# A decode layer's last tile: result halves spread over four quadrants, the last tile in a PSUM tile of its own

## The chip, the cores and the metric

The kernel runs on one core of one Trainium2 chip. The metric is the time of one execution in device microseconds; times are medians of several executions.

## What is computed

One token's layer: a normalized input goes through attention over a window of 4096 cached keys and values (32 query heads, 4 key heads) and through a gated GELU block, and both are added to the input.

```python
x = A_x                                   # [1, 1, 1024]
xn = _layernorm(x, axis=-1)
return x + _A_ref(xn, A_k_cache, A_v_cache, A_wq, A_wo) + _B_ref(xn, B_w_gate, B_w_up, B_w_down)

# _A_ref ends in   o.reshape(1, 1, 4096) @ wo            wo:     [4096, 1024]
# _B_ref ends in   (gelu(x @ w_gate) * (x @ w_up)) @ w_down     w_down: [3584, 1024]
```

All is float32. The result row has 1024 elements and is the sum of x, 4096 rows of wo and 3584 rows of w_down, each weighted by one number.

## The kernel before

Every weight is read once from HBM, as a stream of 24 items (`items`), each of which fills a buffer `chunk` of up to 4 MB; there are four such buffers, so an item is loaded four items ahead, as soon as PE and DVE are done with the buffer's old content. The order of the instructions is that in which the code is written (`manual_schedule`): each engine takes its own in that order, and waits for what it reads.

The change lies in the last eight items: four of wo (kind "o") and four of w_down (kind "d"), of 8 row groups each, 4 in the last. A row group, called a tile t here, is 128 rows of the weight by 1024 columns. A tile is added to the result in one of two ways, in `contract`:
- PE (`accumulate`): four matmuls, one for each quadrant of 32 partitions of the PSUM tile `out_p`. Quadrant c takes 256 columns of the tile, c * 256 to c * 256 + 255 (CO is 256), so `out_p` holds the result row in four pieces in the partitions 0, 32, 64 and 96. A float32 matmul of the code is two MATMUL instructions on the chip, so a tile is eight.
- DVE (`add_scaled`): the tile, scaled by one factor per partition, is added to `out_part`, 128 x 1024 in SBUF. At tile MERGE = 20 of w_down, PE sums `out_part` over the partitions into `out_p` (the matmuls `out_p<-out_part,unit`; called the merge).

Even tiles go to PE and odd ones to DVE, except that from tile 16 of w_down on all go to PE. w_down has 28 tiles, 0 to 27. Tiles 16 to 19 and 20 to 23 are one transfer each (`TAIL`), 24, 25 and 26 one each, and tile 27, the last, comes in two transfers of 512 columns: quadrants 0 and 1 read the first, 2 and 3 the second. Behind it DVE adds `out_p` and `x_out`, the input in the same four pieces (line 453), and SP stores the four pieces (line 454):

```python
nc.vector.tensor_add(y, out_p, x_out)
nc.sync.dma_start(out.rearrange("a b (c n) -> (a b c) n", n=CO), y[0:P:32, :])
```

Of the kernel before, what the change touches and what calls it, by code (L numbers as in the profile page):

```python
# [9 lines left out]
F32 = mybir.dt.float32  # L10
# [5 lines left out]
P = 128  # L16
# [9 lines left out]
CO = D // 4  # L26
TD = DF // P
GROUP = 8
# [3 lines left out]
MERGE = 20  # L32
# [7 lines left out]
def tile_decode_layer(  # L40
# [12 lines left out]
    nc = tc.nc  # L53
    consts = ctx.enter_context(tc.tile_pool(name="consts", bufs=1))
    stream = ctx.enter_context(tc.tile_pool(name="stream", bufs=4))
    work = ctx.enter_context(tc.tile_pool(name="work", bufs=1))
    psum = ctx.enter_context(tc.tile_pool(name="psum", bufs=1, space=PSUM))
# [53 lines left out]
    nc.scalar.dma_start(x_rows, x.rearrange("a b (j p) -> (a b j) p", j=NJ))  # L111
    x_out = work.tile([P, CO], F32, name="x_out")
    nc.vector.memset(x_out, 0.0)
    nc.scalar.dma_start(x_out[0:P:32, :], x.rearrange("a b (c n) -> (a b c) n", n=CO))

    ident = consts.tile([P, P], F32, name="ident")
    make_identity(nc, ident)
# [11 lines left out]
    unit = consts.tile([P, 32], F32, name="unit")  # L129
# [51 lines left out]
    def add_scaled(total, w, factor, first):  # L181

        if first:
            nc.vector.tensor_scalar(total, w, factor, None, op0=ALU.mult)  # L184
        else:
            nc.vector.scalar_tensor_tensor(total, w, factor, total, op0=ALU.mult, op1=ALU.add)  # L186
# [196 lines left out]

    out_p = psum.tile([P, CO], F32, name="out_p", tag="out")
    out_part = work.tile([P, D], F32, name="out_part")

    def accumulate(z, w, start, stop):
        for c in range(4):
            nc.tensor.matmul(  # L389
                out_p[32 * c:32 * c + 32, :], z, w[:, c * CO:(c + 1) * CO], start=start, stop=stop  # L390
            )

    def contract(kind, a, z, count):
        w = loaded.pop((kind, a))
        for i in range(min(GROUP, count - GROUP * a)):
            t = GROUP * a + i
            wt = w[:, i * D:(i + 1) * D]
            if kind == "d" and t == MERGE:
                accumulate(unit, out_part, False, False)
            if i % 2 == 0 or (kind == "d" and t >= MERGE - GROUP // 2):  # L400
                accumulate(z[:, t, :], wt, kind == "o" and t == 0, kind == "d" and t == count - 1)
            else:
                add_scaled(out_part, wt, z[:, t, 0:1], kind == "o" and t == 1)

# [5 lines left out]
    for n, (kind, i) in enumerate(items):  # L410
# [15 lines left out]
        elif kind == "v":  # L426
            vn = loaded.pop(("v", i))
            half = STREAM // 2
            values(2 * i, vn[:, :half])
            values(2 * i + 1, vn[:, half:])  # L430
            if i == 1:
                maxima()
        elif kind in "gu":
            project(kind, i, NA)
            if (kind, i) == ("u", 1):
                state = factors()
            elif (kind, i) == ("u", 2):
                normalizers(*state)
                heads()
        elif kind == "o":  # L440
            if i == 0:
                projected("u", NA)
                gated()
            contract("o", i, oz, HQ)
            if i == 0:
                hidden()
        else:
            contract("d", i, hz, TD)
        if n + ahead < len(items):
            load(n + ahead)  # L450

    y = work.tile([P, CO], F32, name="y")
    nc.vector.tensor_add(y, out_p, x_out)
    nc.sync.dma_start(out.rearrange("a b (c n) -> (a b c) n", n=CO), y[0:P:32, :])


_INS = ["A_x", "A_k_cache", "A_v_cache", "A_wq", "A_wo", "B_w_gate", "B_w_up", "B_w_down"]
# [20 lines left out]
```

## Time and profile before

| | |
|---|---|
| median of 3 runs | 229.94 us (229.8 to 229.94) |
| the profiled execution | 229.72 us |
| its span, first to last instruction | 227.9 us |
| PE, DVE, ACT busy | 123.2, 97.0, 33.3 us |
| HBM read, over the span | 94.38 MB, 414 GB/s |
| last add, last store issued | 224.72 us, 225.17 us |

The span is shorter than the time by what lies around the first and the last instruction, 1.8 us. Times in the rows are counted from the start of the span. PEld is PE's loading of weights, which overlaps PE. SPq is SP's queue, which issues the transfers. In a matmul the small operand of 32 columns (`hz`, `oz`, `unit`) is loaded, and the weight tile streams through.

### The profile page before, as it was taken

The page shows a single profiled execution, that of the slowest core. Times are in us where ns is not written, and L with a number is a line of the kernel's source. Part 1 is how long each engine was busy: PE and PEld are TensorE (multiplying, and loading weights), DVE is VectorE, ACT ScalarE, POOL GpSimd, SP SyncE. Part 2 cuts the span into 40 slices and gives each one's busy share as a digit, 9 for nine tenths or more (in the row PEclk, how much of TensorE's full clock was granted, in tenths as well). Part 3 has the DMA queues.
Part 4 walks back from the last instruction along what each step waited for, and adds up shares of the span by engine and source line. Part 5 has one row for each costly group of instructions (what it writes and reads, how often), then busy time and mean ns, then how long its engine had stood idle before and what let it go on. Part 6 is the DMA issues. An engine that isn't in the chain of part 4 may idle for free.

```text
span 227.9 us, 2497 instructions
## 1 busy us (share of the span) xinstructions
PE 123.2 (54%) x1096; PEld 60.6 (27%) x1096; DVE 97.0 (43%) x103; ACT 33.3 (15%) x57; POOL 0.7 (0%) x6
## 2 busy tenths in 40 slices
PE   1160622567679834269806985384875425063754
PEld 1110000144364701017305472110571202021331
DVE  7340724520204164260380227966817356292600
ACT  2000000054273400006316350000000000000000
POOL 1000000000000000000000000000000000000000
PEclk9999999599958996577975899959655556675879
DMA  7989999999999999999999999999999999999991
GB/s 277 455 380 454 460 391 443 411 456 436 393 440 461 410 410 453 401 438 451 400 428 449 428 424 441 428 443 403 440 454 405 437 449 414 431 443 391 436 378 47
DMA packets 4786, 94.53 MB, mean 415 GB/s; under 512 B 540, under 2 KB 552, under 8 KB 1192
## 3 DMA queue, kind: packets, MB, share of 16 engines
q1 hardware_dynamic: 4760, 94.38, 97.1%
q8 instruction: 8, 0.13, 0.2%
q14 instruction: 2, 0.02, 0.0%
q10 hardware_dynamic: 16, 0.01, 0.0%
HBM read 94.38 MB, written 0.00 MB: 414 GB/s over the span
## 4 chain that ended last, share of the span: by engine, by line
DMA 57%; PE 22%; DVE 11%; ACT 6%; issue 2%; SPq 0%; ACTq 0%; DVEq 0%
DMA chunk<-in_A_k_cache 23%; DMA chunk<-in_B_w_down 15%; DMA chunk<-in_A_wo 14%; PE kt_p L241 8%; DMA chunk<-in_A_wq 5%; PE o_p L278 3%; DVE part L186 3%; PE s_p L250 3%; PE out_p L389 3%; PE acc_q L196 2%; DVE out_part L186 2%; DVE m L253 2%; ACT kT L242 2%; ACT p L256 2%; ACT pT L273 1%
## 5 line engine op out<-in xcount | busy, mean ns | idle before, releaser
L186 DVE SCALAR_TENSOR_TENSOR part<-chunk,xz,part 128x3584 f32<-128x3584 f32 (+1 forms) x9 | 37.1, 4126 | 32.1 <-DMA chunk<-in_A_wq 17.8
L241 PE MATMUL kt_p<-ident,chunk 128*128 128x128 f32 x128 | 23.7, 354 | 15.9 <-ACT kT L242 13.1
L242 ACT ACTIVATE kT<-kt_p 128x512 f32<-128x512 f32 x32 | 18.2, 596 | 70.9 <-PE kt_p L241 70.9
L196 PE MATMUL acc_q<-chunk,xz 128*32 128x512 f32 x64 | 14.3, 1043 | 24.0 <-DMA chunk<-in_A_wq 24.0
L241 PEld LDWEIGHTS kt_p<-ident,chunk 128*128 128x128 f32 x128 | 18.6, 180 | 24.8 <-ACT kT L242 16.2
L389 PE MATMUL out_p<-chunk,hz 128*32 128x256 f32 x160 | 14.8, 530 | 16.5 <-DMA chunk<-in_B_w_down 16.5
L186 DVE SCALAR_TENSOR_TENSOR out_part<-chunk,oz,out_part 128x1024 f32<-128x1024 f32 x15 | 19.3, 1285 | 10.4 <-DMA chunk<-in_A_wo 10.0
L389 PE MATMUL out_p<-chunk,oz 128*32 128x256 f32 x128 | 13.1, 580 | 15.7 <-DMA chunk<-in_A_wo 15.7
L196 PE MATMUL acc_g<-chunk,xz 128*32 128x512 f32 x56 | 10.9, 817 | 11.6 <-DMA chunk<-in_B_w_gate 11.6
L253 DVE TENSOR_REDUCE m<-s_p 128x1 f32<-128x1024 f32 x4 | 4.9, 1222 | 22.0 <-PE s_p L250 22.0
L186 DVE SCALAR_TENSOR_TENSOR out_part<-chunk,hz,out_part 128x1024 f32<-128x1024 f32 x8 | 10.3, 1284 | 9.1 <-DMA chunk<-in_B_w_down 8.9
L389 PEld LDWEIGHTS out_p<-chunk,hz 128*32 128x32 f32 x160 | 6.7, 147 | 24.6 <-DMA chunk<-in_B_w_down 12.5
L196 PEld LDWEIGHTS acc_q<-chunk,xz 128*32 128x32 f32 x64 | 2.5, 159 | 34.2 <-DMA chunk<-in_A_wq 23.3
L389 PEld LDWEIGHTS out_p<-chunk,oz 128*32 128x32 f32 x128 | 5.2, 156 | 23.2 <-DMA chunk<-in_A_wo 18.5
L196 PE MATMUL acc_u<-chunk,xz 128*32 128x512 f32 x56 | 9.4, 713 | 2.6 <-DMA chunk<-in_B_w_up 2.6
L278 PE MATMUL o_p<-chunk,pT 128*32 128x128 f32 x256 | 7.8, 274 | 1.9 <-ACT pT L273 1.9
L250 PE MATMUL s_p<-kT,qz 128*32 128x512 f32 x64 | 8.7, 612 | 0.0
L184 DVE TENSOR_SCALAR part<-chunk,xz 128x3584 f32<-128x3584 f32 (+1 forms) x3 | 6.5, 2169 | 3.9 <-DMA chunk<-in_A_wq 3.9
L278 PEld LDWEIGHTS o_p<-chunk,pT 128*32 128x32 f32 x256 | 6.7, 110 | 2.9 <-ACT pT L273 2.9
L196 PEld LDWEIGHTS acc_g<-chunk,xz 128*32 128x32 f32 x56 | 2.1, 133 | 18.9 <-DMA chunk<-in_B_w_gate 14.5
L256 ACT ACTIVATE p<-s_p,negm 128x1024 f32<-128x1024 f32 x4 | 4.5, 1114 | 8.5 <-DVE negm L254 8.5
L350 DVE TENSOR_TENSOR t_sb<-g_sb 128x512 f32<-128x512 f32 (+1 forms) x2 | 1.4, 686 | 9.8 <-ACT g_sb L349 9.8
(93 smaller groups left out, 73.5 us busy)
## 6 DMA issues: line engine op xcount, KB each, us to landing
chunk<-in_A_wq SPq DMA_DIRECT2D x4, 4096.0 KB, 30.8
chunk<-in_A_wo SPq DMA_DIRECT2D x4, 4096.0 KB, 27.6
chunk<-in_B_w_gate SPq DMA_DIRECT2D x4, 3584.0 KB, 20.5
chunk<-in_B_w_up SPq DMA_DIRECT2D x4, 3584.0 KB, 16.5
chunk<-in_A_k_cache SPq DMA_DIRECT2D x4, 2048.0 KB, 28.3
chunk<-in_A_v_cache SPq DMA_DIRECT2D x4, 2048.0 KB, 28.5
chunk<-in_B_w_down SPq DMA_DIRECT2D x2, 4096.0 KB
chunk<-in_B_w_down SPq DMA_DIRECT2D x2, 2048.0 KB, 30.9
```

The costliest lines, as they stand in the source:

```text
L184: nc.vector.tensor_scalar(total, w, factor, None, op0=ALU.mult)
L186: nc.vector.scalar_tensor_tensor(total, w, factor, total, op0=ALU.mult, op1=ALU.add)
L196: nc.tensor.matmul(acc[kind][32 * c:32 * c + 32, b, :], z, w[:, n * NB:(n + 1) * NB], start=start, stop=stop,)
L241: nc.tensor.transpose(t_p[:, jj * P:(jj + 1) * P], kn[:, j * DH:(j + 1) * DH], ident)
L242: nc.scalar.activation(kT[:, i, :], t_p, AF.Copy)
L250: nc.tensor.matmul(s_p[32 * c:32 * c + 32, b, :], qz[:, g, :], kT[:, i, :], start=True, stop=True)
L253: nc.vector.reduce_max(m[:, g:g + 1], s_p, axis=AX.XY)
L256: nc.scalar.activation(p, s_p, AF.Exp, bias=negm[:, g:g + 1], scale=SCALE, accum_out=l[:, g:g + 1])
L273: nc.scalar.activation(pT[:, b].rearrange("p j q -> p (j q)"), t_p, AF.Copy)
L278: nc.tensor.matmul(o_p[32 * c:32 * c + 32, g, :], pT[:, b, jj, 32 * c:32 * c + 32], vn[:, j * DH:(j + 1) * DH], start=(b == 0 and jj == 0) ...
L350: nc.vector.tensor_mul(ts, gs, gs)
L389: nc.tensor.matmul(out_p[32 * c:32 * c + 32, :], z, w[:, c * CO:(c + 1) * CO], start=start, stop=stop)
```

## The change

The result row is laid out otherwise. Quadrant c now holds 128 columns of each half of the row: h * 512 + c * 128 to h * 512 + c * 128 + 127 for h = 0 and 1. So each of the last tile's two transfers has work for all four quadrants. The load of `x_out` and the store go by the same layout, in eight runs of 128 elements instead of four of 256.

Tile 27 is no longer added to `out_p`. DVE adds `out_p` and `x_out` into `rest` once tile 26 is in, and tile 27 goes into a PSUM tile of its own, `last_p`, in two halves of 128 columns a quadrant; each half is then added to `rest` by DVE. And the rule that all tiles go to PE begins at tile 20 instead of 16, so tiles 17 and 19 are DVE's.

```diff
-    nc.scalar.dma_start(x_out[0:P:32, :], x.rearrange("a b (c n) -> (a b c) n", n=CO))
+    nc.scalar.dma_start(
+        x_out[0:P:32, :].rearrange("c (h n) -> c h n", h=2),
+        x.rearrange("a b (h c n) -> (a b c) h n", h=2, c=4),
+    )
...
-
-    def accumulate(z, w, start, stop):
+    rest = work.tile([P, CO], F32, name="rest")
+    y = work.tile([P, CO], F32, name="y")
+
+    def accumulate(p, z, w, start, stop, halves=slice(0, 2)):
+        w = w.rearrange("p (h c n) -> p c h n", h=2, c=4)
+        o = p.rearrange("p (h n) -> p h n", h=2)
         for c in range(4):
             nc.tensor.matmul(
-                out_p[32 * c:32 * c + 32, :], z, w[:, c * CO:(c + 1) * CO], start=start, stop=stop
+                o[32 * c:32 * c + 32, halves], z, w[:, c, halves], start=start, stop=stop
             )
...
-                accumulate(unit, out_part, False, False)
-            if i % 2 == 0 or (kind == "d" and t >= MERGE - GROUP // 2):
-                accumulate(z[:, t, :], wt, kind == "o" and t == 0, kind == "d" and t == count - 1)
+                accumulate(out_p, unit, out_part, False, False)
+            if kind == "d" and t == count - 1:
+
+                last_p = psum.tile([P, CO], F32, name="last_p", tag="s")
+                nc.vector.tensor_add(rest, out_p, x_out)
+                for h in range(2):
+                    accumulate(last_p, z[:, t, :], wt, True, True, slice(h, h + 1))
+                    cols = slice(h * CO // 2, (h + 1) * CO // 2)
+                    nc.vector.tensor_add(y[:, cols], last_p[:, cols], rest[:, cols])
+            elif i % 2 == 0 or (kind == "d" and t >= MERGE):
+                accumulate(
+                    out_p, z[:, t, :], wt, kind == "o" and t == 0, kind == "d" and t == count - 2
+                )
...
-    nc.vector.tensor_add(y, out_p, x_out)
-    nc.sync.dma_start(out.rearrange("a b (c n) -> (a b c) n", n=CO), y[0:P:32, :])
+    nc.sync.dma_start(
+        out.rearrange("a b (h c n) -> (a b c) h n", h=2, c=4),
+        y[0:P:32, :].rearrange("c (h n) -> c h n", h=2),
+    )
```

On PE the end of the program stands so before, from the transfer of tiles 16 to 19 (DMAHW4) on; each DMAHW is one load's semaphore, a row is a matmul of the code with how many follow each other:

```order
L389 MATMUL out_p<-chunk,hz 32x256 [waits DMAHW4_49]
L389 MATMUL out_p<-chunk,hz 32x256 x15
L389 MATMUL out_p<-out_part,unit 32x256 [waits DVE_49]
...
L389 MATMUL out_p<-chunk,hz 32x256 [waits DMAHW0_49]
L389 MATMUL out_p<-chunk,hz 32x256 x3
L389 MATMUL out_p<-chunk,hz 32x256 [waits DMAHW1_49]
L389 MATMUL out_p<-chunk,hz 32x256
L389 MATMUL out_p<-chunk,hz 32x256 [waits DMAHW2_49]
L389 MATMUL out_p<-chunk,hz 32x256
```

The first two rows are four tiles; DMAHW0 is tile 26, DMAHW1 and DMAHW2 are the halves of tile 27, with two matmuls each. On PE at the same place after the change:

```order
L396 MATMUL out_p<-chunk,hz 32x256 [waits DMAHW4_49]
L396 MATMUL out_p<-chunk,hz 32x256 x7
L396 MATMUL out_p<-out_part,unit 32x256 [waits DVE_49]
...
L396 MATMUL out_p<-chunk,hz 32x256 [waits DMAHW0_49]
L396 MATMUL out_p<-chunk,hz 32x256 x3
L396 MATMUL last_p<-chunk,hz 32x128 [waits DMAHW1_49]
L396 MATMUL last_p<-chunk,hz 32x128 x3
L396 MATMUL last_p<-chunk,hz 32x128 [waits DMAHW2_49,DVE_49]
L396 MATMUL last_p<-chunk,hz 32x128 x3
```

Of tiles 16 to 19 two are left, each half of tile 27 has four matmuls of 128 columns, and the second half waits for DVE beside its DMA. On DVE the end of the program after the change is:

```order
L189 SCALAR_TENSOR_TENSOR out_part<-chunk,hz,out_part 128x1024 [waits DMAHW4_49,DVE_49]
L189 SCALAR_TENSOR_TENSOR out_part<-chunk,hz,out_part 128x1024 [waits DVE_49]
L410 TENSOR_TENSOR rest<-out_p,x_out 128x256 [waits PE_49]
L414 TENSOR_TENSOR y<-last_p,rest 128x128 [waits DVE_49,PE_49]
L414 TENSOR_TENSOR y<-last_p,rest 128x128 [waits PE_49]
```

The first two rows are tiles 17 and 19, new here; the one add of 256 columns at the end has become three, the first of which waits for tile 26 and the other two for a half of tile 27.

## Rows read from the trace of the kernel before

**Rows 1.** The page: span, busy times by engine, DMA's busy tenths by slice

```profile
span 227.9 us, 2497 instructions
...
PE 123.2 (54%) x1096; PEld 60.6 (27%) x1096; DVE 97.0 (43%) x103; ACT 33.3 (15%) x57; POOL 0.7 (0%) x6
...
DMA  7989999999999999999999999999999999999991
```

**Rows 2.** Chain of waits, its end: start, length, what; times in us

```profile
185.72 33.16 DMA chunk<-in_B_w_down
...
218.93 5.77 PE out_p L389 x64
...
224.72 0.43 DVE y L453
```

**Rows 3.** Timeline of 210 to 228: start, length, instruction, [idle time before and its releaser]

```profile
209.17 5.25 DVE L186 SCALAR_TENSOR_TENSOR out_part<-chunk,hz,out_part 128x1024 f32<-128x1024 f32 x4 [4.47 <-DMA chunk<-in_B_w_down]
...
214.02 1.94 PE L389 MATMUL out_p<-chunk,hz 128*32 128x256 f32 x32 [1.25 <-DMA chunk<-in_B_w_down]
...
215.77 0.61 PE L389 MATMUL out_p<-out_part,unit 128*32 128x256 f32 x8
...
222.43 0.22 PEld L389 LDWEIGHTS out_p<-chunk,hz 128*32 128x32 f32 x4 [0.21 <-issue]
222.86 0.22 PEld L389 LDWEIGHTS out_p<-chunk,hz 128*32 128x32 f32 x4 [0.21 <-DMA chunk<-in_B_w_down]
...
224.04 0.14 PEld L389 LDWEIGHTS out_p<-chunk,hz 128*32 128x32 f32 x4 [0.27 <-DMA chunk<-in_B_w_down]
...
225.17 0.63 SPq L454 DMA_DIRECT2D out_y<-y  x1
```

**Rows 4.** Windows: stretch, length, busy PE, PEld, DVE, ACT, POOL; clock, DMA, GB/s

```profile
209.50:212.90 3.40, 3.26 (x32) 1.19 (x24) 3.33 (x3) 0.00 (x0) 0.00 (x0) 0.50 1.03 439
213.00:216.30 3.30, 2.28 (x40) 1.20 (x40) 1.38 (x2) 0.00 (x0) 0.00 (x0) 1.00 0.99 412
216.40:219.70 3.30, 0.77 (x16) 0.52 (x20) 0.00 (x0) 0.00 (x0) 0.00 (x0) 1.00 0.96 395
219.80:223.10 3.30, 3.30 (x36) 1.74 (x32) 0.00 (x0) 0.00 (x0) 0.00 (x0) 0.50 0.87 340
223.20:226.00 2.80, 1.47 (x20) 0.51 (x12) 0.43 (x1) 0.00 (x0) 0.00 (x0) 1.00 0.04 15
```

**Rows 5.** Instructions of lines 389 (from 208 us) and 278: ns min/median/max, first and last start

```profile
L389 PE MATMUL out_p<-chunk,hz x128: 378/506/637, 209.1 to 224.3; 128*32 128x256 f32 x128
...
L278 PE MATMUL o_p<-chunk,pT x256: 272/273/298, 74.9 to 137.6; 128*32 128x128 f32 x128
```

**Rows 6.** Timeline of 223.8 to 224.1, PE

```profile
223.45 1.01 PE L389 MATMUL out_p<-chunk,hz 128*32 128x256 f32 x10
```

**Rows 7.** Groups by form, DVE: count, busy us, mean ns, idle before and its releaser

```profile
L330 DVE TENSOR_TENSOR own<-ot_p,low 128x512 f32<-128x512 f32 x1 | 0.7, 692 | 2.2 <-PE ot_p L325 2.2
L453 DVE TENSOR_TENSOR y<-out_p,x_out 128x256 f32<-128x256 f32 x1 | 0.4, 426 | 10.3 <-PE out_p L389 10.3
```

**Rows 8.** Chain of waits, the matmuls of 128 columns at line 278

```profile
135.90 1.95 PE o_p L278 x64
```

**Rows 9.** Windows further ahead

```profile
154.90:158.30 3.40, 1.92 (x14) 0.41 (x14) 1.37 (x1) 0.00 (x0) 0.00 (x0) 1.00 0.92 395
158.40:161.70 3.30, 1.15 (x24) 0.72 (x28) 2.24 (x4) 0.00 (x0) 0.00 (x0) 1.00 1.05 442
161.80:165.00 3.20, 3.20 (x50) 2.18 (x39) 3.13 (x3) 0.00 (x0) 0.00 (x0) 0.50 1.07 461
```

**Rows 10.** Timeline of SP, the issue of one load and of the last seven

```profile
27.37 0.33 SPq L106 DMA_DIRECT2D chunk<-in_B_w_gate  x1
...
185.34 14.36 SPq L104 DMA_DIRECT2D chunk<-in_B_w_down  x7
```

**Rows 11.** DMA issues: count, KB each, median us to landing

```profile
chunk<-in_B_w_down SPq DMA_DIRECT2D x3, 512.0 KB, 25.6
```

More of the change, by code (lines that the diff above doesn't have):

```diff
@@ L450, in tile_decode_layer @@
             load(n + ahead)
-    y = work.tile([P, CO], F32, name="y")
-    nc.vector.tensor_add(y, out_p, x_out)
-    nc.sync.dma_start(out.rearrange("a b (c n) -> (a b c) n", n=CO), y[0:P:32, :])
+    nc.sync.dma_start(
+        out.rearrange("a b (h c n) -> (a b c) h n", h=2, c=4),
+        y[0:P:32, :].rearrange("c (h n) -> c h n", h=2),
+    )
 _INS = ["A_x", "A_k_cache", "A_v_cache", "A_wq", "A_wo", "B_w_gate", "B_w_up", "B_w_down"]
```

## The prediction

> **What bounds the kernel now.** I read the page first. The DMA engines are busy eight or nine tenths in every slice of the 227.9 us but the first and the last; PE is busy for 54% and DVE for 43% of the span [rows 1]. Up to the last landing the time is the weight stream, and the change touches none of its loads. What can move the end is the stretch behind the last transfers, so I read that next. The chain of waits ends with a load that is in flight for 33.16 us from 185.72 and so lands at 218.88, 5.77 us of PE without a break from 218.93, and the add of 0.43 us [rows 2]. The timeline says more than the chain: PE works through tiles 20 to 27 from 218.93 on, and its last wait is again for a DMA: at 224.04, after 0.27 us of idle weight loads [rows 3]. That is the second half of tile 27. So the last landing and PE end nearly together: a little less PE would gain nothing before 224.04, and a little more would take over. Behind it come 0.66 us of PE (to 224.70), the add at 224.72, and the store, issued at 225.17 [rows 2, 3]. The last 2.7 us, issue and flight of the store, are the same in every case below, so I compare cases by the moment when the store is issued.
>
> The third view is the clock. PE was granted 1.00 (the upper level, 2.4 GHz) from 213.0 to 219.7, 0.50 (1.2 GHz) from 219.8 to 223.1, and 1.00 again behind [rows 4]. A tile is eight instructions, two passes of four that run beside each other in the four quadrants. At the half clock a pass takes 0.43 us (its weight loads stand at 222.43 and 222.86 [rows 3]). At full clock it is 0.22: 32 instructions, eight passes, took 1.94 us [rows 3], of which the last 0.38 is one matmul's own length [rows 5].
>
> **The new order at the end.** Call A the moment when the matmuls of tile 26 end. The ten matmuls that begin at 223.45 [rows 6] are four of tile 26's second pass, four of tile 27's first half and the first two of its second half. So A = 223.45 + 0.02 + 0.38 = 223.85. In the new program five steps follow A, each waiting for the one before, as the order of PE and DVE shows:
> - DVE adds out_p and x_out into rest, 256 columns: 0.43 [rows 7].
> - DVE adds the first half, 128 columns. 512 columns with one operand in PSUM take 692 ns and 256 take 426, so 1.04 ns a column, and 128 cost 0.29 [rows 7].
> - Only then may PE begin the second half: its first matmul waits for the DMA and for DVE. Nothing is queued on PE behind it but this half, and the rest of the kernel waits for that.
> - PE's second half: eight matmuls of 128 columns in place of four of 256. 64 of just this shape took 1.95 us [rows 8] at 0.27 each [rows 5], so they follow each other by (1.95 - 0.27) / 63 = 0.027, and eight take 7 x 0.027 + 0.27 = 0.46.
> - DVE adds the second half: 0.29.
>
> Five hand-overs at 0.02 to 0.05 (between PE and DVE it was 0.02, from DVE's end at 225.15 to SP 0.02 [rows 2, 3]), say 0.04, make 0.20. The sum is 0.43 + 0.29 + 0.46 + 0.29 + 0.20 = 1.67 us from A to the store. The first half of tile 27 is done by then: it follows tile 26 on PE at once and takes about 0.25 us beyond A, inside the 0.47 of the rest.
>
> With A unmoved the store would go out at 223.85 + 1.67 = 225.52, 0.35 later than now. What the change saves behind the last landing (0.66 to 0.46 on PE, 0.43 to 0.29 on DVE) it loses because the 128-column adds and the second half stand in one row instead of side by side. Were there no wait for DVE, the end would be 224.04 + 0.46 + 0.29 + 0.08 = 224.87, 0.30 earlier; that is the lower bound of the edit.
>
> The order shows this wait as it is; a rule of the Trainium skill says why it cannot simply be dropped. In PSUM — Partial Sum Buffer, PSUM bank collisions raise a hardware error, it states that two engines must be kept apart by bank and quadrant, also at disjoint columns. Both halves of last_p lie in the same banks and quadrants. By that rule halves in one tile cannot overlap, which is the 225.52 above and not the 224.87; no run here shows what happens without the guard.
>
> **Two tiles from PE to DVE.** Tiles 17 and 19 leave PE: 16 of the 32 instructions at 214.02, so 0.97 of 1.94 us [rows 3]. DVE gets two adds of the kind of which four took 5.25, 1.31 each. It is free at 209.17 + 5.25 = 214.42 [rows 3], so they end by 217.04, and the merge, which waited for nothing at 215.77, now starts there and takes 0.61, at the half clock about 1.05. It ends by 218.1, before tile 20 lands at 218.88. Both are hidden, with 0.8 us to spare; without that cover each us late would be a us of backlog. No load waits for them: the last ones are issued by 185.34 + 14.36 = 199.7 [rows 10].
>
> But PE's clock can see them. From 213.0 to 216.3 PE now works 2.28 us and the clock stays full [rows 4]. Afterwards it works about 1.05 us there (four passes of 0.22 and what the last matmul's 0.38 reaches beyond), and 0.6 to 1.05 of merge follow after an idle stretch. Nearest rows: 0.77 us stood before the fall at 219.8 and 1.15 before that at 161.8, while 1.92 and 2.28 stood before stretches that stayed full [rows 4, 9]. 1.05 is nearest to those that fell. I take it that PE meets tile 20 at the half clock, and that the clock rises at 223.2 as it does now, since PE is without a break from 218.93 on in both kernels. Then ten passes of 0.43 (tiles 20 to 24) fill 218.93 to 223.2, and the four passes of tiles 25 and 26 follow at 0.22: the last one begins at 223.2 + 3 x 0.22 = 223.86 and ends at 224.26. A is 0.41 later, the store is issued at 225.93, and the sum is +0.76 us. The bounds of this term are 0 (the clock as now) and the half clock up to the end, priced below.
>
> The rows show falls behind idle PE; in TensorE: Matmul & The Clock Gate, HAM oscillation — how this bites in real kernels, the Trainium skill describes the same pattern, bursts of matmuls between waits for DMA that each begin on the low clock. By that rule the thinner burst at 214 makes the half clock at 218.93 the likelier case.
>
> **Edits taken at nothing.** Matmuls of out_p now read two runs of 128 columns. No row has such a read; if each run cost as much as a matmul of its own, 2 x 0.027 = 0.054 an instruction, that is the 0.43 / 8 of today, so 0, and no reason makes it cheaper. The store has eight runs instead of four: four took 0.63 to issue [rows 3], while a load of 128 rows took 0.33 [rows 10], so the number of runs does not set it: 0, within 0.1 either way. The load of x_out in eight runs goes out at the kernel's start and is first read in its last four microseconds: 0.
>
> **The rivals.**
> 1. The clock holds as now, and only the hand-over counts: +0.35, 230.29 us. For it: the present burst, which ends at 216.38, keeps the full clock until PE starts again at 218.93 [rows 2 to 4]. Against it: the halved burst.
> 2. Not slower: PE keeps up with the landings. Place: tiles 24 to 26. If the clock is full there, tile 26 begins when it lands. A tile is 512 KB [rows 11], 0.524 MB, at 395 GB/s [rows 4] 1.33 us, so it lands at 224.02 - 1.33 = 222.69; then A = 222.69 + 0.04 + 0.22 + 0.40 = 223.35 and the store goes out at 225.02: -0.15, 229.79 us. It decides from A below 223.50, which is 225.17 - 1.67. For it: the present margin at 224.04 is only 0.27 us. Against: it wants the full clock well before 223, and PE has shown 3.3 us at half in just that place [rows 4].
> 3. The half clock to the end: 14 passes of 0.43 from 218.93, the last begins at 224.52 and ends 0.66 later (0.64 is the longest matmul [rows 5]), so A = 225.18; with 0.25 more for the second half the store goes at 227.1: +1.9, 231.8 us. Against it: PE is busy without a break, and such a stretch, 209.5 to 212.9, was followed by the full clock [rows 4].
>
> **How the numbers follow.** The sum is made against the profiled execution, 229.72 us for a span of 227.9; the median of the runs shown is 229.94, 0.22 more, and I add to the median. Forecast: 229.94 + 0.76 = 230.7, chance 0.50. Rival 1: 0.25; rival 2: 0.15; rival 3: 0.10. A measurement tells about 0.2%, 0.46 us, from no change. The forecast's clock term runs from 0 upwards, so 0.08 of its 0.50 falls under 0.46; with rival 3 and 0.01 of rival 1 that makes slower 0.53. Rival 2 gives 0.05 to faster: its 0.15, the 0.1 of the store and the 0.14 by which the runs shown differ come near 0.46; same has 0.42. The range from 229.7 to 231.3 takes in rival 2 (229.79), rival 1 and a rise of the clock 1.2 us later than now (half of that, 0.6, on the forecast); it leaves out the lower bound of the edit and most of rival 3.
>
> **What would show it.** In the new profile: the second half's first matmul waits for DVE and not for a DMA; the adds of 128 columns take 0.29 and the eight matmuls 0.46; 1.67 us from tile 26's end to the store; PE's clock at 0.50 from 218.9 on, and tile 26 ending after 224. The hand-over step is wrong if the last wait on PE is the DMA's; the clock step is wrong if the clock is 1.00 when tile 20 begins or if PE idles between tiles 24 and 26. A later last landing or a store of other length would put it all wrong.

## The result, and the profile after

The changed kernel takes 230.69 us (median of 15 executions, 229.96 to 231.58), the kernel before 229.80 in the same series (229.66 to 230.11). The medians differ by 0.89 us, slower; the ratio, which takes in all executions and is not the quotient of the two medians, is 1.0041 [1.003, 1.0052]. Its executions lie 1.62 us apart, those of before 0.45. The profiled execution of the changed kernel took 230.22 us, 0.50 more than that of before but 0.47 less than its own median; so the trace shows a good execution, and a part of the loss has to be found in other runs.

The page of the kernel after, span and busy times:

```profile
span 228.4 us, 2488 instructions
...
PE 127.5 (56%) x1088; PEld 62.7 (27%) x1088; DVE 100.1 (44%) x107; ACT 33.6 (15%) x57; POOL 0.7 (0%) x6
```

PE has eight instructions fewer than before and is busy for 4.3 us more [rows 1]; the mean of its granted clock over the span was 0.716, and 0.790 before. The windows of the kernel after (start:end, length, busy PE, PEld, DVE, ACT, POOL with counts, granted clock, DMA share, GB/s) say where that was at the end:

```profile
213.00:216.30 3.30, 1.07 (x16) 0.42 (x16) 3.19 (x4) 0.00 (x0) 0.00 (x0) 0.89 0.99 412
216.40:219.70 3.30, 1.86 (x16) 0.60 (x20) 0.58 (x1) 0.00 (x0) 0.00 (x0) 0.50 0.96 391
219.80:222.30 2.50, 2.50 (x28) 1.13 (x24) 0.00 (x0) 0.00 (x0) 0.00 (x0) 0.50 0.94 365
222.40:226.00 3.60, 2.08 (x44) 0.97 (x36) 1.01 (x3) 0.00 (x0) 0.00 (x0) 1.00 0.14 53
```

Before, the clock was still 1.00 from 216.4 to 219.7 and 0.50 behind [rows 4]. Now PE works 1.07 us from 213.0 to 216.3 where it worked 2.28. The clock falls behind that burst (0.89 is the mean of the stretch), is at the half before tile 20 begins, and is full again from about 222.4.

The timeline of the kernel after (start, length, engine, line, instruction, count, idle time before and what ended it):

```profile
211.73 5.25 DVE L189 SCALAR_TENSOR_TENSOR out_part<-chunk,hz,out_part 128x1024 f32<-128x1024 f32 x4
...
213.94 1.07 PE L396 MATMUL out_p<-chunk,hz 128*32 128x256 f32 x16 [1.46 <-DMA chunk<-in_B_w_down]
...
217.04 1.08 PE L396 MATMUL out_p<-out_part,unit 128*32 128x256 f32 x8 [2.03 <-DVE out_part L189]
...
218.92 4.91 PE L396 MATMUL out_p<-chunk,hz 128*32 128x256 f32 x56 [0.80 <-DMA chunk<-in_B_w_down]
...
224.79 0.43 PE L396 MATMUL last_p<-chunk,hz 128*32 128x128 f32 x8 [0.73 <-DVE y L414]
225.28 0.29 DVE L414 TENSOR_TENSOR y<-last_p,rest 128x128 f32<-128x128 f32 x1 [0.55 <-PE last_p L396]
225.60 0.68 SPq L469 DMA_DIRECT2D out_y<-y  x1
```

Three things are to be seen. The adds of tiles 17 and 19 end at 216.98 and the merge, at the half clock, lies from 217.04 to 218.12, before tile 20 lands. PE's last wait is no longer for a DMA [rows 3] but for DVE. And the store goes out at 225.60 against 225.17 [rows 3]. The end of the chain of waits in the kernel after (start, length, what) is one row of work, as the order had it:

```profile
218.92 4.97 PE out_p L396 x56
223.89 0.02 issue
223.91 0.44 DVE rest L410
...
224.44 0.30 DVE y L414
224.74 0.04 issue
224.79 0.47 PE last_p L396 x8
225.26 0.02 issue
225.28 0.29 DVE y L414
```

A, the end of tile 26, is 218.92 + 4.97 = 223.89, and from there to the store it takes 1.71 us.

### The profile page after: what moved, and what is told of

Read it like the earlier page. It is cut to its first block, busy times and chain, and to the rows that moved or that the text cites. A ratio compares the mean times of both kernels' runs of the same rounds, so it can differ in the third digit from the quotient of the medians.

```text
span 228.4 us, 2488 instructions
## 1 busy us (share of the span) xinstructions
PE 127.5 (56%) x1088; PEld 62.7 (27%) x1088; DVE 100.1 (44%) x107; ACT 33.6 (15%) x57; POOL 0.7 (0%) x6
## 4 chain that ended last, share of the span: by engine, by line
DMA 56%; PE 23%; DVE 12%; ACT 5%; issue 2%; SPq 0%; ACTq 0%; DVEq 0%
DMA chunk<-in_A_k_cache 21%; DMA chunk<-in_B_w_down 15%; DMA chunk<-in_A_wo 15%; PE kt_p L244 9%; DMA chunk<-in_A_wq 5%; PE o_p L281 3%; DVE part L189 3%; PE s_p L253 3%; PE acc_q L199 2%; DVE out_part L189 2%; PE out_p L396 2%; DVE m L256 2%; ACT p L259 2%; ACT kT L245 1%; PE q_p L222 1%
## 5 line engine op out<-in xcount | busy, mean ns | idle before, releaser
L244 PE MATMUL kt_p<-ident,chunk 128*128 128x128 f32 x128 | 25.8, 379 | 14.3 <-ACT kT L245 11.6
L244 PEld LDWEIGHTS kt_p<-ident,chunk 128*128 128x128 f32 x128 | 20.6, 195 | 24.5 <-ACT kT L245 14.9
L396 PE MATMUL out_p<-chunk,oz 128*32 128x256 f32 x128 | 14.1, 618 | 15.3 <-DMA chunk<-in_A_wo 15.3
L396 PE MATMUL out_p<-chunk,hz 128*32 128x256 f32 x136 | 13.1, 553 | 14.4 <-DMA chunk<-in_B_w_down 14.4
L189 DVE SCALAR_TENSOR_TENSOR out_part<-chunk,hz,out_part 128x1024 f32<-128x1024 f32 x10 | 12.8, 1285 | 9.2 <-DMA chunk<-in_B_w_down 8.9
L396 PEld LDWEIGHTS out_p<-chunk,hz 128*32 128x32 f32 x136 | 5.6, 152 | 22.7 <-issue 11.5
L253 PE MATMUL s_p<-kT,qz 128*32 128x512 f32 x64 | 10.2, 713 | 0.0
```

The lines of the kernel that those rows point to most:

```text
L244: nc.tensor.transpose(t_p[:, jj * P:(jj + 1) * P], kn[:, j * DH:(j + 1) * DH], ident)
L253: nc.tensor.matmul(s_p[32 * c:32 * c + 32, b, :], qz[:, g, :], kT[:, i, :], start=True, stop=True)
L396: nc.tensor.matmul(o[32 * c:32 * c + 32, halves], z, w[:, c, halves], start=start, stop=stop)
```

## The experiments

In the table "to before" is the difference of the medians, each against the kernel before in runs on the same chip (before: 229.76 to 229.80 each time). The last two columns are of the profiled execution: the granted clock from 219 to 222 us, where tiles 20 to 23 are worked through, and the moment when the last store is issued.

| kernel | median, us | to before | ratio, 95% | lowest to highest | clock 219 to 222 | last store |
|---|---|---|---|---|---|---|
| before | 229.80 | | | 0.45 | 0.63 | 225.17 |
| after | 230.69 | +0.89 | 1.0041 [1.003, 1.0052] | 1.62 | 0.50 | 225.60 |
| e1_pe_tiles | 230.03 | +0.27 | 1.0012 [1.0003, 1.0021] | 0.78 | 1.00 | 225.30 |
| e2_two_banks | 229.88 | +0.12 | 1.0008 [0.9997, 1.0019] | 1.16 | 0.50 | 225.75 |
| e3_both | 229.59 | -0.17 | 0.999 [0.9981, 0.9999] | 0.32 | 0.50 | 225.06 |
| e6_warm | 229.85 | +0.09 | 1.0006 [0.9997, 1.0015] | 0.63 | 1.00 | 225.10 |
| e4_dve_tiles | 230.23 | +0.45 | 1.0018 [1.0008, 1.0027] | 0.92 | 0.50 | 225.66 |
| e5_layout | 229.66 | -0.12 | 0.9993 [0.9984, 1.0002] | 0.36 | 1.00 | 224.98 |
| e7_rest_early | 229.75 | -0.03 | 0.9998 [0.9989, 1.0007] | 0.64 | 1.00 | 224.96 |
| e9_two_stores | 229.69 | -0.09 | 0.9998 [0.999, 1.0007] | 0.91 | 0.50 | 225.24 |
| e10_both_again | 229.63 | -0.15 | 0.9993 [0.9984, 1.0002] | 0.48 | 1.00 | 224.86 |
| e11_early_again | 229.58 | -0.20 | 1.0 [0.9987, 1.0012] | 1.35 | 0.72 | 224.96 |

The theory is that of the forecast: two costs that add up, the row of steps behind the wait for DVE, and the half clock that meets tile 20 because tiles 17 and 19 have left PE. The rivals are the one without the other, and a third cause in the layout (reads of two runs, the store in eight).

**Tiles 17 and 19 back on PE.** The wait for DVE stays.

```diff
-            elif i % 2 == 0 or (kind == "d" and t >= MERGE):
+            elif i % 2 == 0 or (kind == "d" and t >= MERGE - GROUP // 2):
```

> The changed kernel with tiles 17 and 19 back on PE; everything else of the change stays. Theory (hand-over plus clock): the burst at 214 us is whole again, so PE meets tile 20 at 218.9 us at the full clock as in the kernel before, and only the hand-over is left: 0.35 to 0.45 us over before, about 230.2 us, and the runs lie close together (within 0.5 us, against 1.6 us in the changed kernel). Rival (the clock has no part, all comes from the hand-over and the new layout): no change against the changed kernel, 230.7 us, runs as far apart as there.

The time is +0.27 to before, a little under the 0.35 to 0.45 expected, so 0.62 of the 0.89 hangs on which engine has the two tiles. The executions lie 0.78 apart, more than the 0.5 expected. The timeline of e1_pe_tiles:

```profile
214.18 3.64 PE L396 MATMUL out_p<-chunk,hz 128*32 128x256 f32 x32 [1.27 <-DMA chunk<-in_B_w_down]
...
222.91 0.64 PE L396 MATMUL out_p<-chunk,hz 128*32 128x256 f32 x8 [0.62 <-DMA chunk<-in_B_w_down]
...
224.49 0.43 PE L396 MATMUL last_p<-chunk,hz 128*32 128x128 f32 x8 [0.51 <-DVE y L414]
...
225.30 0.68 SPq L469 DMA_DIRECT2D out_y<-y  x1
```

In this execution PE is at the half clock at 214 (32 instructions take 3.64 us, not 1.94), where it harms nothing, and at the full clock from 219 on. So tile 20 met the full clock as expected, but not behind a burst at the full clock. Tile 26 then begins when it lands, at 222.91. This is rival 2's place, PE keeping up, and still the store is later than before: the wait for DVE alone holds the second half until 224.49.

**A second PSUM tile, one for each half.** The wait for DVE goes, since PE and DVE then never hold the same tile; tiles 17 and 19 stay on DVE.

```diff
+                last_q = psum.tile([P, CO], F32, name="last_q", tag="o")
...
-                    accumulate(last_p, z[:, t, :], wt, True, True, slice(h, h + 1))
+                    own = (last_p, last_q)[h]
+                    accumulate(own, z[:, t, :], wt, True, True, slice(h, h + 1))
...
-                    nc.vector.tensor_add(y[:, cols], last_p[:, cols], rest[:, cols])
+                    nc.vector.tensor_add(y[:, cols], own[:, cols], rest[:, cols])
```

> The changed kernel with a PSUM tile of its own for each half of tile 27, so that PE's second half does not wait for DVE; tiles 17 and 19 stay on DVE. Theory (hand-over plus clock): from the end of tile 26 to the store it takes 0.43 + 2 x 0.29 + about 0.12 = 1.15 us in place of 1.74, unless the last landing ends later, so about 0.5 us under the changed kernel: 230.2 us, with runs still about 1.3 us apart. Rival (the wait for DVE costs nothing, the second half's DMA is as late): 230.7 us.

It came out at +0.12, lower than expected. The timeline of e2_two_banks:

```profile
219.13 5.49 PE L396 MATMUL out_p<-chunk,hz 128*32 128x256 f32 x56 [0.74 <-DMA chunk<-in_B_w_down]
...
224.67 0.39 PE L396 MATMUL last_q<-chunk,hz 128*32 128x128 f32 x8
224.71 0.42 DVE L411 TENSOR_TENSOR rest<-out_p,x_out 128x256 f32<-128x256 f32 x1 [7.45 <-PE out_p L396]
...
225.75 0.68 SPq L471 DMA_DIRECT2D out_y<-y  x1
```

Both halves are on PE before DVE has made rest. From the start of that add it is 1.04 us to the store; in after it was 225.60 - 223.91 = 1.69. So the wait costs 0.65 us when PE is late. And PE is late here: this execution (230.37 us) met tile 20 at the half clock, and rest begins 0.80 later than in after, 0.21 of it because tile 20 itself began later (219.13 against 218.92). In PSUM — Partial Sum Buffer, PSUM bank collisions raise a hardware error, the Trainium skill states that accesses of two engines to different banks go on side by side; the trace agrees, the matmuls of the second half at 224.67 lie beside DVE's add at 224.71.

**Both together.**

> Both edits: tiles 17 and 19 on PE, and a PSUM tile for each half. Theory: tile 26 ends at about 223.85 as in the kernel before, the store is issued 1.15 later at 225.0 in place of 225.17: 229.65 us, 0.15 under the kernel before, runs close together. Rival (the new layout costs by itself: matmuls that read two runs, a store of eight runs): 229.9 to 230.3 us, over the kernel before.

e3_both has both diffs above. At -0.17 [0.9981, 0.9999] it is the only kernel whose interval lies below 1, if by little. Its second half waits for the DMA again, as its timeline shows:

```profile
224.25 0.42 PE L396 MATMUL last_q<-chunk,hz 128*32 128x128 f32 x8 [0.22 <-DMA chunk<-in_B_w_down]
```

With e1, e2 and after this makes a square of four:

| to before, us | wait for DVE | two PSUM tiles | difference |
|---|---|---|---|
| tiles 17 and 19 on DVE | +0.89 (after) | +0.12 (e2) | 0.77 |
| on PE | +0.27 (e1) | -0.17 (e3) | 0.44 |
| difference | 0.62 | 0.29 | |

Each of the two parts costs by itself, and together more than the sum. With PE early the second half can't begin before its landing anyway, at 224.04 in e5 below and 224.25 in e3, so the wait costs less: 0.44 by the medians, 0.24 by the traced executions (225.30 against 225.06). With PE late it costs the whole 0.65. The 0.77 of the medians is more than that; the medians of kernels whose executions lie 1.16 and 1.62 apart are not sure to a tenth, and we leave it there.

**Work put back on PE that nobody reads.** e6_warm is the changed kernel, wait and DVE tiles and all, with matmuls of tiles 16 to 18 into a PSUM tile of their own ahead of the merge and of tile 16 once more behind it. They add 32 instructions to PE.

```diff
+            if kind == "d" and MERGE - 4 <= t < MERGE:
+                held.append(wt)
...
+                fill_p = psum.tile([P, CO], F32, name="fill_p", tag="acc")
+                for n in range(3):
+                    accumulate(fill_p, z[:, MERGE - 4 + n, :], held[n], True, True)
                 accumulate(out_p, unit, out_part, False, False)
+                for n in range(1):
+                    accumulate(fill_p, z[:, MERGE - 4 + n, :], held[n], True, True)
```

> The changed kernel with idle work for PE: three tiles' worth of matmuls before the merge and one behind it, on data that is there, into a PSUM tile that nobody reads; the result is computed as before. Theory (the clock is set by what PE does before tile 20): PE is at the full clock when tile 20 comes, works through tiles 20 to 26 as they land or with a short backlog, and the time falls by 0.4 to 0.9 us to 229.8 to 230.25 us; the granted clock is 1.00 around 219 us. Rival (the clock is not moved by such work, or the backlog has another cause): 230.7 us or more, since the added work can only delay PE.

With more work on PE the time falls from +0.89 to +0.09 and the distance between executions from 1.62 to 0.63. The windows of e6_warm:

```profile
213.00:216.30 3.30, 2.32 (x40) 1.20 (x40) 3.19 (x4) 0.00 (x0) 0.00 (x0) 1.00 0.99 412
216.40:218.80 2.40, 1.07 (x16) 0.42 (x16) 0.62 (x1) 0.00 (x0) 0.00 (x0) 1.00 0.94 389
219.00:222.00 3.00, 2.81 (x48) 1.24 (x47) 0.00 (x0) 0.00 (x0) 0.00 (x0) 1.00 1.00 393
```

and its timeline:

```profile
214.87 1.48 PE L396 MATMUL fill_p<-chunk,hz 128*32 128x256 f32 x24
...
217.08 0.64 PE L396 MATMUL out_p<-out_part,unit 128*32 128x256 f32 x8 [0.73 <-DVE out_part L189]
...
217.53 0.61 PE L396 MATMUL fill_p<-chunk,hz 128*32 128x256 f32 x8
...
223.41 0.43 DVE L419 TENSOR_TENSOR rest<-out_p,x_out 128x256 f32<-128x256 f32 x1 [6.39 <-PE out_p L396]
...
225.10 0.68 SPq L478 DMA_DIRECT2D out_y<-y  x1
```

The clock is 1.00 from 213 on, rest begins 0.50 earlier than in after (223.41 against 223.91), and from there it is again 1.69 us to the store. The wait for DVE, the two tiles on DVE and the late merge are all still there. So the price of the two DVE tiles is not their work, nor anything in the DMA or the merge, but the clock at which PE meets the last tiles; that the ten executions without a trace had the full clock too is inferred from their times. In TensorE: Matmul & The Clock Gate, HAM oscillation — how this bites in real kernels, the Trainium skill advises, for bursts of matmuls between waits for DMA, to do more of them ahead of a wait so that PE keeps its upper clock; the trace of e6 agrees, 1.00 in place of 0.50.

**The two tiles alone, in the kernel before.**

```diff
-            if i % 2 == 0 or (kind == "d" and t >= MERGE - GROUP // 2):
+            if i % 2 == 0 or (kind == "d" and t >= MERGE):
```

> The kernel before with one edit: tiles 17 and 19 go to DVE. Layout, out_p, the one add and the store are as before, and nothing on PE waits for DVE at the end. Theory (the thinner burst lowers the clock that PE has for tiles 20 to 27): PE is behind the landings at the end in most runs, and the end moves by 0 to 0.9 us from run to run: median 230.0 to 230.2 us, runs about 1 us apart, against 0.4 us in the kernel before. Rival (the two tiles are harmless by themselves, DVE's 2.6 us and PE's merge being hidden): 229.8 us, runs close together.

Measured +0.45 [1.0008, 1.0027], 230.23 us and so just above the 230.0 to 230.2 expected, with executions 0.92 apart. The windows of e4_dve_tiles:

```profile
213.00:216.30 3.30, 1.94 (x16) 0.59 (x16) 3.19 (x4) 0.00 (x0) 0.00 (x0) 0.50 0.97 407
...
219.00:222.00 3.00, 3.00 (x32) 1.39 (x36) 0.00 (x0) 0.00 (x0) 0.00 (x0) 0.50 1.01 396
...
223.00:224.00 1.00, 1.00 (x16) 0.41 (x11) 0.00 (x0) 0.00 (x0) 0.00 (x0) 0.50 0.19 72
224.00:225.00 1.00, 1.00 (x20) 0.36 (x12) 0.00 (x0) 0.00 (x0) 0.00 (x0) 0.96 0.00 0
```

the last burst in its chain of waits:

```profile
218.98 6.20 PE out_p L389 x64
```

and the store in its timeline:

```profile
225.66 0.62 SPq L454 DMA_DIRECT2D out_y<-y  x1
```

Here the backlog is seen whole: half clock from tile 20 to about 224, the same 64 instructions in 6.20 us, not 5.77 [rows 2], and the store 0.49 later at no change of layout. The half clock came by another road than in after: it was there at 214 already, the 16 instructions of the burst took 1.94 us and not 1.07, and behind them the clock stayed where it was. In e1 PE was at the half clock at 214 too, and behind 32 instructions there and the merge it met tile 20 at the full one.

**The layout alone.** Tile 27 goes into out_p in halves, one add of 256 columns ends the program, and tiles 17 and 19 stay on PE.

```diff
-                last_p = psum.tile([P, CO], F32, name="last_p", tag="s")
-                nc.vector.tensor_add(rest, out_p, x_out)
                 for h in range(2):
-                    accumulate(last_p, z[:, t, :], wt, True, True, slice(h, h + 1))
...
+                    accumulate(out_p, z[:, t, :], wt, False, h == 1, slice(h, h + 1))
+                nc.vector.tensor_add(y, out_p, x_out)
...
```

> The new layout alone: each half of tile 27 gives four matmuls of 128 columns, but into out_p itself; one add of 256 columns at the end as in the kernel before; tiles 17 and 19 on PE. Theory: from the last landing to the store 0.04 + 0.46 + 0.04 + 0.43 + 0.03 = 1.00 us in place of 1.17, and the store of eight runs 0.07 longer: 229.7 us, 0.1 under the kernel before. Rival (matmuls that read two runs are slower): 229.8 us or more.

Measured -0.12 [0.9984, 1.0002]: no cost of the layout is seen, and it may gain a little, so the third cause falls. The timeline of e5_layout:

```profile
218.93 2.37 PE L396 MATMUL out_p<-chunk,hz 128*32 128x256 f32 x40 [0.65 <-DMA chunk<-in_B_w_down]
...
224.04 0.42 PE L396 MATMUL out_p<-chunk,hz 128*32 128x128 f32 x8 [0.21 <-DMA chunk<-in_B_w_down]
224.53 0.42 DVE L410 TENSOR_TENSOR y<-out_p,x_out 128x256 f32<-128x256 f32 x1 [10.12 <-PE out_p L396]
224.98 0.68 SPq L465 DMA_DIRECT2D out_y<-y  x1
```

Ten passes with reads of two runs take 2.37 us at the full clock, 9 x 0.216 and one matmul's own length of about 0.4: no dearer than the reads of one run [rows 3]. Of e3's gain the own PSUM tiles then bring 0.05 beyond this, which these runs cannot tell from nothing.

**Two tries to get more out of e3.** In e7_rest_early tile 26 too goes into last_p and last_q, so that rest is made a tile earlier. e9_two_stores has the same early rest, and each half has a y and a store of its own, the first from ACT's queue, the second from SP's.

```diff
+            if kind == "d" and t == count - 2:
                 nc.vector.tensor_add(rest, out_p, x_out)
+                own = [
+                    psum.tile([P, CO], F32, name="last_p", tag="s"),
+                    psum.tile([P, CO], F32, name="last_q", tag="o"),
+                ]
+                for h in range(2):
+                    accumulate(own[h], z[:, t, :], wt, True, False, slice(h, h + 1))
+            elif kind == "d" and t == count - 1:
+                for h in range(2):
+                    accumulate(own[h], z[:, t, :], wt, False, True, slice(h, h + 1))
...
+                    nc.vector.tensor_add(y[:, cols], own[h][:, cols], rest[:, cols])
```

```diff
+    for h, queue in enumerate((nc.scalar, nc.sync)):
+        queue.dma_start(rows_out[:, h], y_half[h][0:P:32, :])
```

> Tiles 17 and 19 on PE, a PSUM tile of its own for each half, and tile 26 goes into these two as well, so that DVE's add of 256 columns comes after tile 25 and lies ahead of the last landings. Theory: the store goes out 0.04 + 0.46 + 0.04 + 0.29 + 0.03 = 0.86 us after the last landing whatever the backlog of DVE, as the kernel with two PSUM tiles already showed in its profile: 229.5 to 229.6 us, the same as that one or up to 0.1 better in its slower runs. Rival (something else than the adds holds the store): no better than 229.59 us.

> The kernel with the early add, and a store of its own for each half: ACT issues that of the first half, SP that of the second, four runs of 128 elements each. Theory: the store of eight runs took 0.05 us longer to issue and 0.07 to the end; with four runs on the path this comes back, and the first store is hidden: 229.45 to 229.5 us. Rival (the end of the kernel waits for two stores, and the second engine adds its own hand-over): 229.6 us or more.

Neither gained beyond e3, and both missed what was expected: 229.75 and 229.69 us, -0.03 and -0.09, both with 1 in their intervals. The reason shows in the timeline of e7_rest_early:

```profile
224.15 0.43 PE L396 MATMUL last_q<-chunk,hz 128*32 128x128 f32 x8 [0.22 <-DMA chunk<-in_B_w_down]
```

and of e9_two_stores:

```profile
224.43 0.42 PE L396 MATMUL last_q<-chunk,hz 128*32 128x128 f32 x8 [0.16 <-DMA chunk<-in_B_w_down]
224.67 0.59 ACTq L477 DMA_DIRECT2D out_y<-y  x1
224.92 0.29 DVE L420 TENSOR_TENSOR y<-last_q,rest 128x128 f32<-128x128 f32 x1 [0.28 <-PE last_q L396]
225.24 0.63 SPq L477 DMA_DIRECT2D out_y<-y  x1
```

Once the second half waits for its DMA, all that stands behind the landing is 0.49 of PE, 0.32 of DVE and the store; rest was made in time already, and a first store that goes out while PE is still at the second half doesn't bring the second one forward. From the start of the second half to the last store it is 0.81 us in e3, e7 and e9 alike. So their traced stores differ only by when the last load lands (224.25, 224.15 and 224.43). What is left to win lies in the store: 0.05 of its issue (0.63 for four runs, 0.68 for eight), and from its issue to the end of the span about 2.7 us in e9 (227.9 - 225.24) against 2.8 in e7 (227.8 - 224.96). The later landing of e9's execution hides it, and the medians do not show it.

**Both again, and e7 again,** side by side on one chip, since e3 and e7 had run on two.

> The kernel with tiles 17 and 19 on PE and a PSUM tile for each half, once more, beside the kernel with the early add on the same chip. Theory (both kernels end 0.86 us after the last landing, and their difference of 0.16 us was a matter of when the last load landed): both within 0.1 us of each other, 0.1 to 0.25 us under the kernel before. Rival (the early add costs something on PE or DVE): this one again 0.15 us under the other.

> The kernel with the early add once more. Theory: within 0.1 us of the kernel without it. Rival: 0.15 us over it, near the kernel before.

They are the kernels of e3 and e7 unchanged, and came out at -0.15 and -0.20, no different from each other. Two of e11's eleven executions took 230.71 and 230.78, which is why its ratio is 1.0 though its median is the lowest; why they did, stays open. The pair e3 and e10 shows more: one program, two executions, two places of the half clock. The windows of e3_both,

```profile
213.00:216.30 3.30, 2.26 (x40) 1.20 (x40) 1.40 (x2) 0.00 (x0) 0.00 (x0) 1.00 0.98 412
...
219.00:222.00 3.00, 2.87 (x28) 1.38 (x32) 0.00 (x0) 0.00 (x0) 0.00 (x0) 0.50 1.00 395
222.00:223.00 1.00, 1.00 (x24) 0.52 (x20) 0.00 (x0) 0.00 (x0) 0.00 (x0) 1.00 0.62 238
```

and of e10_both_again:

```profile
213.00:216.30 3.30, 2.28 (x24) 1.14 (x28) 1.38 (x2) 0.00 (x0) 0.00 (x0) 0.50 1.00 422
...
219.00:222.00 3.00, 2.81 (x48) 1.29 (x48) 0.00 (x0) 0.00 (x0) 0.00 (x0) 1.00 1.00 393
```

and its second half in the timeline:

```profile
224.05 0.42 PE L396 MATMUL last_q<-chunk,hz 128*32 128x128 f32 x8 [0.23 <-DMA chunk<-in_B_w_down]
```

In e3 the half clock lies on tiles 20 to 23, in e10 on the burst at 214. So what a kernel does ahead decides only in part; the place differs from one execution to the next. In these two executions the place costs nothing: both second halves wait for the DMA, and the stores, at 225.06 and 224.86, lie as far apart as the landings, 0.20.

## Why the prediction was right, point by point

The forecast was +0.76, the measurement +0.89, and the range held it. By its steps:

- **From A to the store,** 1.67: right in kind, 1.71 in size. From the start of rest to the store it was 1.69 in after, e1 and e6 alike. By the chain the four steps took 0.44, 0.30, 0.47 and 0.29, together 1.50 where 1.47 was derived, and the five hand-overs 0.21 where 0.20 was taken. These were uneven: from rest to the add of the first half, both on DVE, 0.09 passed and not 0.04, and the others took 0.02 to 0.05.
- **The second half waits for DVE and not for a DMA:** right. The other bound of this edit, a store at 224.87 were there no wait, came true in e10: 224.86.
- **Tiles 17 and 19 hidden:** right to a tenth. The merge was to lie from 217.04 to 218.1 and lay from 217.04 to 218.12.
- **The half clock meets tile 20:** right in after, e2 and e4, the three profiled kernels whose burst at 214 is halved without filling (in e4 the clock was at the half before that burst too). With all four tiles on PE it lay on tiles 20 to 23, wholly or in part, in four profiled executions of eight (before, e3, e9, e11; not in e1, e5, e7, e10). So the two tiles moved the odds rather than switched the clock, and a single trace of before could not tell that. Three traces against eight would not show it by themselves; the times of e1, e4 and e6 do.
- **The clock rises at 223.2 as before, so A is 0.41 later:** the place failed in the traced execution. The clock rose there at about 222.4, and A was 223.89 against 223.85, not after 224 as the prediction's own sign for this step asks. The 0.50 of that execution is the hand-over's 1.71 - 1.32 = 0.39, 0.07 of the store and 0.04 of A: rival 1's sum, though by another road. The rise at 223.2 was one execution's; in e4 it was at about 224.
- **0.35 and 0.41 add up:** near in size, +0.76 against +0.89 in the median, and in part by luck, for the runs show no fixed price for either term. The two tiles cost 0.62 with the wait (after less e1), 0.29 without it (e2 less e3) and 0.45 in the layout of before (e4). The wait costs 0.77 with the tiles on DVE and 0.44 with them on PE. And e6, which has the wait, the store and the tiles on DVE but PE at the full clock, measured +0.09 and not 0.46: its A was 223.39, 0.46 ahead of that of before. So 0.39 and 0.07 hold for a given A, and the rest of the 0.89 is how much later A comes in the median execution, which no trace shows.
- **Reads of two runs at nothing:** right (e5). **The store within 0.1:** right, at about 0.07: 0.05 more to issue, and from its issue to the span's end 2.8 us in place of 2.7 (228.4 - 225.60 against 227.9 - 225.17).
- **Rival 2,** PE keeping up and -0.15: PE did keep up in e1 and e6, and the time was not below before. Its step was A = 223.35 (it was 223.59 and 223.39) and 1.67, and it left out the store; with 1.71 and 0.07 it comes to -0.04 at its best A, and e6 measured +0.09.
- **Rival 3,** the half clock to the end, +1.9: in no median. The slowest executions of after, 231.52 to 231.58, come near its 231.8, but they weren't traced.

What the prediction did not foresee is the spread of 1.62 us. That it comes from where the half clock falls is argued, from e3 and e10, from e6's smaller spread, and from rises seen between 222 and 224; the slow executions themselves have no trace here. It would also say why before has only 0.45: there the landing at 224.04 holds the end, so an earlier A gains nothing [rows 3], while in after every shift of A goes on to the store.

The best version is e3_both, the new layout with a PSUM tile for each half and tiles 17 and 19 on PE. Its ratio to before is 0.999 [0.9981, 0.9999], and 0.9993 [0.9984, 1.0002] when run again (e10). It is clearly faster than after, and some 0.15 us faster than before, at the limit of what can be told: the second interval has 1 in it.

## What to carry to other kernels

Cutting the tail of a kernel into halves gains only if the halves can overlap. If the last add is cut too, give each half a PSUM tile of its own, or the second half waits for the reader of the first. That wait cost 0.44 us by the medians with PE early and 0.65 by the traces with PE late, more than the 0.34 that the halving saves behind the last landing by the prediction's terms. Or leave the add whole: e5 did, in one PSUM tile, and came as low within what can be told. Taking work off an engine ahead of its last burst isn't free even where the taken work is hidden, because a TensorE with less to do ahead may meet the burst at half its clock; look at the granted clock of the stretch, and price the burst at both levels. And where a cost hangs on the clock, one trace is one draw: compare medians and spreads of several executions before settling its size.

## What the runs showed of the hardware that was not expected

- One program met the same stretch at 0.50 in one execution and at 1.00 in another (e3, e10). Their clocks differed before it too, 1.00 and 0.50 at 214, while PE and DVE had the same work.
- Matmuls that nobody reads made a kernel faster: 32 more instructions on PE, 0.80 us less against before (+0.89 to +0.09).
- A pass of four matmuls of 256 columns follows the last by 0.43 us at the half clock and 0.22 at the full one, whether its reads are one run or two; on DVE an add that needs the one before it starts 0.09 us behind it, and a hand-over between PE and DVE takes 0.02 to 0.05.
- The issue of the store depends a little on its runs: 0.63 us for four of 256 elements [rows 3] and for four of 128 (e9), 0.68 for eight of 128.
